# Output products of a strided plane made for two batches at once, with a new order of steps

## The chip, the core and the metric

The kernel runs on one NeuronCore of one Trainium2 chip. The metric is device time in microseconds of one execution. The engines are named as in the profile: PE (TensorE, matmuls; PEld are its weight loads), DVE (VectorE), ACT (ScalarE), POOL (GpSimd) and SP (SyncE, which only issues transfers here). Each engine works through its own list of instructions in order and waits on semaphores for the others.

## What is computed

Linear attention with a learned feature map, followed by a gated causal convolution unit. Cut to what matters:

```python
batch, n_heads, seq, head_dim, d_feat = 8, 8, 576, 64, 128

def phi(x):                                     # x: q or k
    proj = np.einsum('bhsd,df->bhsf', x, w_phi)
    proj = proj - np.max(np.abs(proj), axis=-1, keepdims=True)
    return np.concatenate([np.exp(proj), np.exp(-proj)], axis=-1)

q_p, k_p = phi(q), phi(k)
kv = np.einsum('bhsf,bhsd->bhfd', k_p, v)
z = np.sum(k_p, axis=2)
num = np.einsum('bhsf,bhfd->bhsd', q_p, kv)
den = np.einsum('bhsf,bhf->bhs', q_p, z)[..., None] + 1e-06
x = (num / den).transpose(0, 2, 1, 3).reshape(8, 576, 512)

gate_pre = sum(conv_w[t] * xp[:, t:t + 576] for t in range(5))   # causal, xp is x padded by 4
out = (1 / (1 + np.exp(-gate_pre)) * (x @ w_val)) @ w_out
```

## The kernel before

**Tiling.** Row s of a sequence is split as s = 9 r + j, with r from 0 to 63 and j from 0 to 8: nine "planes" j of 64 rows each. The work is cut into 32 units, four per batch, each a pair of heads on the 128 partitions. Planes 0 to 7 of a unit are handled together, two planes per product. Plane 8 of a batch is left over; it is done once per batch, for all eight heads, by the steps whose names begin with h.

**Steps of a unit.** T transposes k and q on PE into PSUM, Tc copies them to on-chip memory (Tk, Tq, Tkc and Tqc are the halves for unit 0). PK and PA project k and q with tokens on the partitions. mK and mQ take the maximum magnitude per row on DVE, NG negates it on POOL, and E takes its exponential on ACT. Kp and Km are the two exponentials of the keys on ACT; V scales v by E on POOL; KV is the product of keys and values on PE, and KM its copy. PQ projects q with features on the partitions, SH subtracts the maxima there by a product with a negative identity, Qp and Qm are the two exponentials. NUM is numerator and denominator, XN the division on DVE. XQ (PE transposes) with XC (a copy), or XP (a transposing transfer on SP's queue), turn the result to have channels on the partitions, in one of two XT buffers.

**Steps of a batch.** HL copies a one-row shifted edge inside XT on POOL. GA makes the convolution as products with diagonal matrices DIAG, built once by DG0 to DG3 from the taps (CW holds them); TH is the tanh of the gate, VAa and VAb are the value products, GV is the gated value on DVE, OUT the output products, four of 128x512 per group of 128 rows, OE the eviction with a factor of one half, ST the stores. For plane 8 the same is done by hGA, hVA, hTH, hGV, hOUT, hOE and hST. LX and LY make a permuted copy of the output weights, WX one of the value weights.

**Where plane 8's output products stand.** A batch has only 64 rows in plane 8. hOUT therefore makes 64 output partitions at a time: for each of four blocks of input channels two products, one for each half of the output columns, with the halves on partitions 0 to 63 and 64 to 127 of one bank:

```python
PS[x * 64:x * 64 + 64, bank[0], 0:256],
m.hGV[:, jt // 2, (jt % 2) * R:(jt % 2 + 1) * R], wout(jt, x * 256, x * 256 + 256),
```

**Order.** A string, ORDER, lists every step with its number, its PSUM banks after @ and, where there is a choice, its engine after a colon (P is POOL, D DVE, A ACT, S SP). The program issues the steps in that order, so it sets the order on every engine. `Lk`, `Lq` and `Lv` are loads of a batch: a single digit is the batch, 11 is plane group 1 of batch 0, 12 groups 2 and 3; LV and LO load the two weight matrices. POOL issues most of them, so they take places in POOL's list. Z1 is a filler: one product of zeros that keeps PE busy. Steps that read the same PSUM banks on two engines keep the order of the list.

## Time and profile before

| | us |
|---|---|
| runs shown | 228.06, 228.54, 232.13 |
| median of these | 228.54 |
| the profiled execution | 227.52 |
| span of its records | 225.7 |

The profile shows the profiled execution only, by the span's own clock from 0. A group's row gives its count, its busy time and the mean of one instruction in ns, then the idle time of the engine just before it and what ended that. "Busy" of PE includes the pipelined end of each matmul, so neighbouring groups overlap. The chain of waits is followed back from the last instruction; each piece in it has its start, its length, and its engine, tile and line.

### The profile page before, as it was taken

How to read it: one execution, taken by the hardware profiler on the slowest of the kernel's cores; microseconds unless marked ns; L12 is line 12 of the kernel's file. 1: busy time of each engine (PE TensorE's matmuls, PEld its weight loads, DVE VectorE, ACT ScalarE, POOL GpSimd, SP SyncE). 2: the span in 40 equal slices, each digit the busy share in tenths (PEclk: the TensorE clock that was granted, in tenths of full speed). 3: DMA queues.
4: the chain of work that ended last, by engine and by line, in shares of the span. 5: the costliest groups of instructions: out<-in, count | busy, mean ns of one | idle time of the engine just before them, and what ended most of it. 6: DMA issues, size and time to landing. Idle time of an engine off the chain costs nothing.

```text
span 225.7 us, 10552 instructions
## 1 busy us (share of the span) xinstructions
PE 208.0 (92%) x4667; PEld 137.0 (61%) x4667; DVE 182.9 (81%) x291; ACT 190.0 (84%) x290; POOL 120.1 (53%) x177
## 2 busy tenths in 40 slices
PE   7738898999999999998998999999999999999991
PEld 2325666666757556755756676766675677577550
DVE  1699989988997998969895999889976998683361
ACT  3488999999999898897996899899999989979241
POOL 7198986664876338726646427832672564640101
PEclk9967999999999999999999999999999999999999
DMA  6999998060994993519998994089427545600456
GB/s 178 262 209 207 207 208 143 6 105 8 161 156 99 174 165 78 126 24 162 186 132 225 140 126 124 9 157 180 72 36 126 121 89 126 156 13 3 112 125 184
DMA packets 30823, 28.90 MB, mean 128 GB/s; under 512 B 12245, under 2 KB 25941, under 8 KB 30778
## 3 DMA queue, kind: packets, MB, share of 16 engines
q0 software_dynamic: 13024, 14.45, 41.5%
q1 hardware_dynamic: 17290, 13.19, 26.9%
q8 instruction: 36, 0.59, 1.1%
q10 hardware_dynamic: 464, 0.59, 1.0%
q14 instruction: 9, 0.07, 0.1%
HBM read 30.48 MB, written 9.44 MB: 177 GB/s over the span
## 4 chain that ended last, share of the span: by engine, by line
PE 60%; DVE 9%; ACT 9%; DMA 9%; issue 8%; POOL 2%; POOLq 0%; SPq 0%; DVEq 0%; ACTq 0%
PE PS L854 10%; PE PS L890 8%; PE PS L380 7%; PE PS L514 6%; PE PS L608 5%; PE PS L537 5%; DMA XT<-XN 4%; PE PS L822 4%; DMA kN<-in_k_dram 3%; PE PS L328 3%; ACT QT L581 3%; PE PS L528 3%; ACT KT L465 3%; DMA out_dram<-hOS 2%; DVE MQ L395 2%
## 5 line engine op out<-in xcount | busy, mean ns | idle before, releaser
L487 POOL TENSOR_TENSOR VT<-vN,E 128x1024 bf16<-128x1024 bf16 x28 | 53.3, 1905 | 29.1 <-ACT E L442 28.8
L465 ACT ACTIVATE KT<-PS 128x1024 bf16<-128x1024 f32 x64 | 64.0, 1036 | 2.8 <-DVE MK L395 1.5
L581 ACT ACTIVATE QT<-PS 128x1024 bf16<-128x1024 f32 x64 | 62.3, 1032 | 4.6 <-PE PS L537 4.6
L395 DVE TENSOR_REDUCE MK<-PS 128x8 f32<-128x1024 f32 x32 | 39.0, 1220 | 8.9 <-PE PS L380 5.3
L395 DVE TENSOR_REDUCE MQ<-PS 128x8 bf16<-128x1024 f32 x32 | 38.9, 1217 | 0.8 <-PE PS L380 0.5
L890 PE MATMUL PS<-WOX,GV 128*128 128x512 bf16 x96 | 26.0, 379 | 0.0
L436 POOL TENSOR_SCALAR MK<-MK 128x8 f32<-128x8 f32 x32 | 7.5, 236 | 34.6 <-DVE MK L395 28.9
L380 PE MATMUL PS<-W,T 64*128 64x128 bf16 x512 | 24.4, 220 | 1.3 <-DVE T L207 0.7
L854 PE MATMUL PS<-XT,WVX 128*128 128x512 bf16 x96 | 24.7, 380 | 0.4 <-issue 0.2
L514 PE MATMUL PS<-VT,KT 64*128 64x65 bf16 x1024 | 22.5, 191 | 1.7 <-DVE XN L619 0.5
L880 DVE SCALAR_TENSOR_TENSOR GV<-GATE,PS 128x512 bf16<-128x512 bf16 x32 | 21.0, 681 | 2.9 <-PE PS L854 2.4
L619 DVE TENSOR_TENSOR XN<-PS,RCP 128x512 bf16<-128x512 f32 x32 | 22.1, 691 | 1.3 <-DVE RCP L618 0.2
L514 PEld LDWEIGHTS <-KT 64*128 64x128 bf16 x1024 | 19.0, 94 | 6.5 <-issue 1.4
L380 PEld LDWEIGHTS <-T 64*128 64x128 bf16 x512 | 16.1, 95 | 9.7 <-issue 5.2
L608 PE MATMUL PS<-KVS,QT 128*128 128x65 bf16 x512 | 21.5, 193 | 0.1
L608 PEld LDWEIGHTS <-QT 128*128 128x128 bf16 x512 | 19.3, 98 | 3.3 <-issue 1.5
L537 PE MATMUL PS<-nident,MQ 128*128 128x128 bf16 x256 | 19.8, 220 | 0.0
L832 ACT ACTIVATE GATE<-PS 128x1024 bf16<-128x1024 f32 x15 | 14.6, 1031 | 5.6 <-PE PS L822 5.6
L207 DVE COPY T<-PS 128x1024 bf16<-128x1024 bf16 (+1 forms) x25 | 16.8, 673 | 2.4 <-PE PS L328 2.3
L537 PEld LDWEIGHTS <-MQ 128*128 128x128 bf16 x256 | 14.4, 98 | 5.6 <-issue 4.4
L890 PEld LDWEIGHTS <-GV 128*128 128x128 bf16 x128 | 11.1, 97 | 10.8 <-DVE GV L880 0.4
L618 DVE RECIPROCAL RCP<-PS 128x8 f32<-128x8 f32 (+1 forms) x40 | 7.9, 198 | 10.1 <-PE PS L608 9.5
(100 smaller groups left out, 390.5 us busy)
## 6 DMA issues: line engine op xcount, KB each, us to landing
out_dram<-OS SPq DMA_DIRECT2D x28, 256.0 KB, 3.9
qN<-in_q_dram POOLq DMA_DIRECT2D x7, 576.0 KB, 9.2
kN<-in_k_dram POOLq DMA_DIRECT2D x7, 576.0 KB, 7.8
vN<-in_v_dram POOLq DMA_DIRECT2D x7, 576.0 KB, 7.8
vF<-in_v_dram SPq DMA_DIRECT2D x2, 576.0 KB, 8.5
out_dram<-hOS SPq DMA_DIRECT2D x14, 64.0 KB, 3.2
out_dram<-OS SPq DMA_DIRECT2D x6, 128.0 KB, 2.5
WVAL<-in_moe_w_val_dram POOLq DMA_DIRECT2D x1, 512.0 KB, 12.1
```

The lines of the kernel that those rows point to most:

```text
L380: nc.tensor.matmul(PS[:, bank[jj], x * P:(x + 1) * P], t(r, x), W2[r, :], start=True, stop=True,)
L395: nc.vector.tensor_reduce(dst, x, AX.X, ALU.max, apply_absolute_value=True)
L465: nc.scalar.activation(o, x, AF.Exp, scale=1.0 if ft == 0 else -1.0)
L487: e.tensor_tensor(dst[:, :, :, 0:D], x.unsqueeze(1).to_broadcast([P, 2, n, D]), E[:, :, :].unsqueeze(3).to_broadcast([P, 2, n, D]), ALU.mult,)
L514: nc.tensor.matmul(PS[:, bank[h], ft * E1:(ft + 1) * E1], w, x, start=(c == 0), stop=(c == 8),)
L537: nc.tensor.matmul(PS[:, u.PQ[jj], :].rearrange("p (h x r) -> p h x r", h=2, x=4)[:, :, x, :], u.MQ[:, jj, x:x + 1].to_broadcast([P, P]), ...
L581: nc.scalar.activation(o, x, AF.Exp, scale=1.0 if ft == 0 else -1.0)
L608: nc.tensor.matmul(PS[:, bank[x // 2], y * E1:(y + 1) * E1], u.QT[:, ft, h * 4 + x, :, :].rearrange("p j r -> p (j r)"), u.KVS[:, h, ft * ...
L619: nc.vector.tensor_tensor(dst, nv[:, :, :, 0:D], rv.unsqueeze(3).to_broadcast([P, n, 4, D]), ALU.mult,)
L854: nc.tensor.matmul(PS[:, m.val[jt], :], wval(dt, jt), XTs[m.b % 2][:, dt, 4 * R:12 * R], start=(dt == 0), stop=(dt == 3),)
L880: nc.vector.scalar_tensor_tensor(out=m.GV[:, jt, :], in0=m.GATE[:, jt, :], scalar=1.0, in1=PS[:, m.val[jt], :], op0=ALU.add, op1=ALU.mult,)
L890: nc.tensor.matmul(PS[:, m.out[x], :], m.GV[:, jt, x * P:(x + 1) * P], wout(jt), start=(jt == 0), stop=(jt == 3),)
```

## The change

Batches 0 to 5 are taken in pairs (PAIRED = 3 pairs). Both batches of a pair write their gated plane 8 into one tile, hGV, laid out so that for each block of 128 channels the 64 rows of the even batch and the 64 of the odd one are next to each other. The odd batch's step hOUTm then makes four products of 128x512 for both, hOEm evicts 128x512 in one step into a tile of its own pool, and hSTm stores it by two transfers of 64 rows with all 512 columns. hOUT, hOE and hST of batches 0 to 5 are gone; batches 6 and 7 keep theirs. `seen`, `behind`, `between` and the steps SHt and hSHt are added to the code, but no step of the list uses them.

```diff
@@ op_hGV
-        m.hGV = pools["hGV"].tile([P, 2, 2 * R], BF16, name="hGV")
+        if PAIRED and b % 2 and b < 2 * PAIRED:
+            m.hGV = batches[b - 1].hGV
+        else:
+            m.hGV = pools["hGV"].tile([P, 2, 2, 2, R], BF16, name="hGV")
+        o = m.hGV[:, :, :, b % 2, :]
+        g = m.hGATE[:, :, :].rearrange("p a (c r) -> p a c r", r=R)
+        v = banks(m.hG)[:, :, 2 * R:4 * R].rearrange("p a (c r) -> p a c r", r=R)
         nc.vector.scalar_tensor_tensor(
-            out=m.hGV[:, :, :], in0=m.hGATE[:, :, :], scalar=1.0, in1=banks(m.hG)[:, :, 2 * R:4 * R],
-            op0=ALU.add, op1=ALU.mult,
+            out=o, in0=g, scalar=1.0, in1=v, op0=ALU.add, op1=ALU.mult,
         )
@@ op_hOUT
-                    m.hGV[:, jt // 2, (jt % 2) * R:(jt % 2 + 1) * R], wout(jt, x * 256, x * 256 + 256),
+                    m.hGV[:, jt // 2, jt % 2, b % 2, :], wout(jt, x * 256, x * 256 + 256),
@@ new steps
+    def op_hOUTm(b, bank):
+        m = batches[b]
+        m.hout = bank[0]
+        for jt in range(4):
+            nc.tensor.matmul(
+                PS[:, bank[0], :], m.hGV[:, jt // 2, jt % 2, :, :].rearrange("p b r -> p (b r)"), wout(jt),
+                start=(jt == 0), stop=(jt == 3),
+            )
+
+    def op_hOEm(b, eng):
+        m = batches[b]
+        m.hOS = pools["hOSm"].tile([P, DM], FP32, name="hOSm")
+        half(eng, m.hOS[:, :], PS[:, m.hout, :])
+
+    def op_hSTm(b, eng):
+        for x in range(2):
+            engines[eng].dma_start(
+                out[b - 1 + x].rearrange("(r j) o -> r j o", j=J)[:, 8, :],
+                batches[b].hOS[x * 64:x * 64 + 64, :],
+            )
@@ ORDER, its first two lines
-XZ0:D Z1@0 Z1@0 Lq11:P Z1@0 Z1@0 Z1@0 Z1@0 Z1@0 Z1@0 Lk11:P Z1@0 CK0 Tk0@0,1 W0 Z1@2 Z1@2 CQ0 Z1@2
-Tq0@2,3 Lv13:S Tqc0:D Tkc0:A PA0@0,1 PK0@2,3 LC0 ND0:D Lk12:P Lv12:S T1@4,5 mQ0 mK0 Lq12:P PQ0@6,7
+Z1@0 Z1@0 XZ0:D Z1@0 Lk11:P CQ0 Z1@0 ND0:D Z1@0 Z1@0 Z1@0 XZ1:D Lq11:P Z1@0 Z1@0 CK0 Z1@0 Z1@0 W0 Z1@0
+Z1@0 Tk0@0,1 Lv13:S Tq0@2,3 Z1@4 LC0 Z1@4 Tkc0:D Tqc0:D Z1@7 PQ0@0,1 PA0@2,3 mQ0 PK0@6,7 Km0 Lk12:P
```

ORDER is a new list throughout: the steps keep their meaning, but their places, banks and, for 41 of them, their engines differ. Fillers number 28 in place of 27. Among the steps that change engine: Tkc0, Tc1, KM0, LY3, hTc1 and XC0 go from ACT to DVE, hTc0 and WX2 from DVE to ACT, DG1 and WX1 from DVE to POOL, WX3 from POOL to ACT. The rest are evictions and copies that change sides between ACT and DVE in both directions.

DVE's list at the start of the program, before. MQ and MK are the maxima, W the projection weights, T and hT the transposed inputs, DIAG the diagonal matrices, cwT the taps.

```order
L226 CAST kN<-kF 128x576
L232 CAST W_161<-wtmp 128x128
L207 COPY T<-PS 128x2x4x64
L220 TENSOR_SCALAR nident<-ident_bf 128x128
L395 TENSOR_REDUCE MQ<-PS 128x8
L395 TENSOR_REDUCE MK<-PS 128x8
L207 CAST ident_159<-ident_bf 5x5
L395 TENSOR_REDUCE MK<-PS 128x8
L395 TENSOR_REDUCE MQ<-PS 128x8
L245 TENSOR_SCALAR cwT<-PS 128x20
L260 TENSOR_TENSOR DIAG<-ident_bf,cwT 128x5x32 x4
L207 COPY hT<-PS 128x512
```

The same place now:

```order
L226 CAST kN<-kF 128x576
L232 CAST W_164<-wtmp 128x128
L207 COPY T<-PS 128x2x4x64 x2
L395 TENSOR_REDUCE MQ<-PS 128x8
L207 COPY T<-PS 128x2x8x64
L207 CAST ident_162<-ident_bf 5x5
L395 TENSOR_REDUCE MK<-PS 128x8 x2
L245 TENSOR_SCALAR cwT<-PS 128x20
L395 TENSOR_REDUCE MQ<-PS 128x8
L207 COPY T<-PS 128x2x8x64
L395 TENSOR_REDUCE hMQ<-PS 128x4
```

Both halves of unit 0's transposes and those of unit 1 are copied by DVE now, and the DIAG row and the copy of hT have left this place.

POOL's list for the first units, before. VT and hVT are the scaled values of V and hV, vF is batch 0's v, the 128x16 and 128x8 casts belong to V and hV.

```order
L487 TENSOR_TENSOR VT<-vF,E 128x16x64
L491 CAST VT<-E 128x16
L272 DMA qN<-in_q_dram 128x4x576
L272 DMA vN<-in_v_dram 128x4x576
L687 TENSOR_SCALAR hMK<-hMK 128x4
L272 DMA vN<-in_v_dram 128x4x576
L487 TENSOR_TENSOR hVT<-vF,hE 128x8x64
L491 CAST hVT<-hE 128x8
L487 TENSOR_TENSOR VT<-vF,E 128x16x64
L491 CAST VT<-E 128x16
L260 TENSOR_TENSOR DIAG<-ident_bf,cwT 128x5x32 x4
L260 TENSOR_TENSOR DIAG<-ident_bf,cwT 128x5x64 x2
```

The same place now:

```order
L487 TENSOR_TENSOR VT<-vF,E 128x16x64
L491 CAST VT<-E 128x16
L260 TENSOR_TENSOR DIAG<-ident_bf,cwT 128x640
L487 TENSOR_TENSOR VT<-vF,E 128x16x64
L491 CAST VT<-E 128x16
L260 TENSOR_TENSOR DIAG<-ident_bf,cwT 128x5x32 x4
L707 TENSOR_SCALAR hMK<-hMK 128x4
L260 TENSOR_TENSOR DIAG<-ident_bf,cwT 128x5x64 x2
L487 TENSOR_TENSOR hVT<-vF,hE 128x8x64
L491 CAST hVT<-hE 128x8
```

Three groups of DIAG (DG0, DG3, DG2) now stand ahead of hV0, which stood before them; the loads that stood here have moved ahead of the first V.

POOL's list around unit 13, before; numbers are those of the tiles. VT_2330, VT_2484 and VT_2615 are the values of units 12, 13 and 14, hVT_2421 those of plane 8 of batch 3; XT0_168 is the edge copy of batch 2.

```order
L487 TENSOR_TENSOR VT_2330<-vN_351,E_2274 128x16x64
L491 CAST VT_2330<-E_2274 128x16
L436 TENSOR_SCALAR MK_2291<-MK_2291 128x8
L487 TENSOR_TENSOR hVT_2421<-vN_351,hE_2319 128x8x64
L491 CAST hVT_2421<-hE_2319 128x8
L487 TENSOR_TENSOR VT_2484<-vN_351,E_2413 128x16x64
L491 CAST VT_2484<-E_2413 128x16
L436 TENSOR_SCALAR MK_2474<-MK_2474 128x8
L207 COPY XT0_168<-XT0_168 128x4x4x63
L487 TENSOR_TENSOR VT_2615<-vN_351,E_2521 128x16x64
```

The same place now; VT_2489 belongs to unit 13 and VT_2579 to unit 14:

```order
L487 TENSOR_TENSOR VT_2489<-vN_1432,E_2384 128x16x64
L491 CAST VT_2489<-E_2384 128x16
L272 DMA qN_2495<-in_q_dram 128x4x576
L436 TENSOR_SCALAR MK_2487<-MK_2487 128x8
L207 COPY XT0_173<-XT0_173 128x4x4x63
L487 TENSOR_TENSOR VT_2579<-vN_1432,E_2524 128x16x64
```

The load of batch 4's q, which had stood behind unit 10's values, now stands behind unit 13's.

## The prediction, made before the changed kernel ran

> **What bounds the kernel now.** I read the page's head first, then busy time by stage, then what the matmul engine waits for between the start and the last batch, then the chain of waits and the order of time in the first 30 us. The page:

> ```profile
> span 225.7 us, 10552 instructions
> PE 208.0 (92%) x4667; PEld 137.0 (61%) x4667; DVE 182.9 (81%) x291; ACT 190.0 (84%) x290; POOL 120.1 (53%) x177
> PE 60%; DVE 9%; ACT 9%; DMA 9%; issue 8%; POOL 2%; POOLq 0%; SPq 0%; DVEq 0%; ACTq 0%
> ```

> PE carries 60% of the chain that ends last. Three stretches by busy time (the columns are the stretch, PE, PEld, DVE, ACT, POOL, PE's clock), and the sum of the six batches between the first tap products of batch 0 and those of batch 6:

> ```profile
> 0.00:22.60 22.60, 15.30 (x221) 8.27 (x222) 15.24 (x25) 14.07 (x21) 15.20 (x27) 0.85 1.05 214
> 22.60:45.10 22.50, 20.00 (x497) 14.48 (x494) 21.58 (x38) 22.00 (x34) 17.31 (x28) 1.00 0.83 141
> 203.10:225.70 22.60, 17.79 (x254) 10.13 (x252) 8.72 (x18) 9.35 (x17) 2.04 (x5) 0.99 0.42 106
> sum 148.91, PE 145.91 PEld 97.56 DVE 131.24 ACT 137.34 POOL 79.77; mean PE 24.32 PEld 16.26 DVE 21.87 ACT 22.89 POOL 13.30
> ```

> So there are two limits. In the middle PE works 145.91 of 148.91 us: only PE work that is taken out, or a new PE wait, moves the end. In the start it is ACT and DVE: from 22.6 to 45.1 us ACT works 22.00 of 22.50, DVE 21.58, while PE has gaps. What the start gains is passed to the end, because PE runs without a hole from there. The longest wait of PE from 40 to 212 us:

> ```profile
> PE PS L822 <- issue: 0.6, 1, 0.6
> ```

> No PE wait there is longer than 0.6 us, so there is no stall in the middle for a new order to remove.

> **The change, part by part.** First the matmuls of plane 8. The chain of waits has hOUT (eight 64-column products), an ordinary OUT (four of 128x512, the shape that hOUTm has) and, from a closer window of the same chain, one filler product of zeros:

> ```profile
> 90.64 0.56 PE PS L977 x8
> 91.81 0.86 PE PS L890 x4
> 125.71 0.32 PE PS L213
> ```

> Six hOUT cost 6 x 0.56 = 3.36 us, three hOUTm 3 x 0.86 = 2.58: PE loses 0.78 us, all in the stretch where PE is the limit. Against it the new list has one filler more among the PE-bound batches (four in place of three after the first tap products): +0.32. Together -0.46.

> [...]

> The evictions:

> ```profile
> L903 ACT ACTIVATE OS<-PS 128x512 f32<-128x512 f32 x14 | 8.4, 624 | 2.8 <-PE PS L890 2.8
> L903 ACT ACTIVATE hOS<-PS 128x256 f32<-128x256 f32 x6 | 2.4, 401 | 0.7 <-PE PS L977 0.5
> L905 DVE TENSOR_SCALAR hOS<-PS 128x256 f32<-128x256 f32 x2 | 0.8, 413 | 0.0
> ```

> Six hOE were four on ACT and two on DVE (4 x 0.40 + 2 x 0.41); three hOEm on ACT are 3 x 0.62. ACT +0.27, DVE -0.83, neither on the path in the middle; if they were, -0.83 to +0.27 bounds it, and I take 0. The hGV write now goes in runs of 64 with a gap: no row shows such a write. Its price lies between 0 and, if gaps doubled it, 8 x 0.4 us on DVE; it resembles most the same shape without gaps, and I take 0, covered by the 17.7 us that DVE is idle in the 148.91. The stores are six fewer on SP's queue, with the same bytes; SP waits for data most of the time, so 0, between a fraction of a microsecond gained and lost at the end of the last store, which isn't one of them.

> Now the start. Its pieces in order of time (the chain first: DG1, and batch 0's tap products, which end the start; then single instructions, with the idle time before them and who ended it in square brackets):

> ```profile
> 13.39 2.74 DVE DIAG L260 x4
> 46.65 1.28 PE PS L822 x80
> ```
> ```profile
> 1.17 4.02 PE L213 MATMUL PS<-zt 128*128 128x512 bf16 x9 [1.17 <-DVE zt L173]
> 5.71 1.26 PE L213 MATMUL PS<-zt 128*128 128x512 bf16 x3
> 13.35 0.23 ACT L442 ACTIVATE E<-MK 128x16 f32<-128x16 f32 x1
> 16.52 0.39 PE L380 MATMUL PS<-W,hT 64*128 64x128 bf16 x4 [2.24 <-DVE hT L207]
> 17.68 1.08 ACT L700 ACTIVATE hKT<-PS 128x512 bf16<-128x512 f32 x2 [1.37 <-DVE hMK L395]
> 29.53 1.94 ACT L581 ACTIVATE QT<-PS 128x1024 bf16<-128x1024 f32 x2
> 90.73 0.26 POOL L491 CAST VT<-E 128x16 bf16<-128x16 f32 x1
> ```

> In the old order DG1 holds DVE for 2.74 us from 13.39, hTc0 stands behind it, PE then waits 2.24 us and ACT 1.37. The new order builds DG1 on POOL in unit 4 and copies hTc0 on ACT. The prices of the copies that change engines:

> ```profile
> L205 ACT ACTIVATE T<-PS 128x1024 bf16<-128x1024 bf16 x7 | 7.2, 1028 | 3.0 <-PE PS L328 3.0
> L205 ACT ACTIVATE KVS<-PS 128x260 bf16<-128x260 f32 x20 | 7.9, 397 | 3.2 <-PE PS L514 2.7
> L205 ACT ACTIVATE XT<-PS 128x512 bf16<-128x512 bf16 x6 | 3.7, 614 | 0.0
> L205 ACT ACTIVATE XT<-PS 128x256 bf16<-128x256 bf16 x5 | 1.9, 387 | 0.0
> L205 ACT ACTIVATE hT<-PS 128x512 bf16<-128x512 bf16 x3 | 1.8, 604 | 0.0
> L205 ACT ACTIVATE WOX<-PS 128x512 bf16<-128x512 f32 x1 | 0.7, 666 | 0.0
> L207 DVE COPY WVX<-WVAL 128x256 bf16<-128x256 bf16 x2 | 1.7, 883 | 0.0
> L207 DVE COPY WVX<-WVAL 128x128 bf16<-128x128 bf16 x4 | 0.8, 252 | 0.0
> L207 DVE COPY T<-PS 128x512 bf16<-128x512 bf16 x1 | 0.4, 424 | 1.4 <-PE PS L328 1.4
> L260 POOL TENSOR_TENSOR DIAG<-ident_bf,cwT 128x160 bf16<-128x160 bf16 x4 | 1.7, 447 | 0.0
> L260 POOL TENSOR_TENSOR DIAG<-ident_bf,cwT 128x320 bf16<-128x320 bf16 x2 | 1.4, 714 | 0.0
> L260 POOL TENSOR_TENSOR DIAG<-ident_bf,cwT 128x640 bf16<-128x640 bf16 x1 | 1.2, 1246 | 0.0
> L487 POOL TENSOR_TENSOR VT<-vF,E 128x1024 bf16<-128x1024 f32 x4 | 7.8, 1939 | 1.1 <-ACT E L442 1.1
> ```

> I follow ACT up to the end of unit 3's query exponentials (31.47 now), where ACT has no hole left. From its list go KM0 (0.40), LY3 (0.67), hTc1 (0.60) and XC0 (0.61), 2.28 us; hTc0 (0.60) and WX2 come. No row shows WX2 on ACT: two ACT copies of 256 columns are 0.77, two of DVE's are 1.77; it reads on-chip memory as the second does, but runs on the engine of the first, so I take 0.8. Net -0.9. The copies Tc1 (1.03) and Tkc0 (0.6) leave ACT too, but there ACT had nothing else ready: I cost that at 0. The 1.37 us wait goes. What is late instead: four more fillers of 0.43 each (1.26 / 3) stand ahead of the first transposes, but the three that stood between the two halves now stand behind both, so the second half comes as early as before; then both halves are copied on DVE one after the other (0.42 more) and the first maxima start about 0.5 later. And hE0 on ACT now waits for hNG0, which stands on POOL behind DG3: about 0.6. So -0.9 - 1.37 + 0.5 + 0.6 = -1.2. WX2's dearer price would leave -0.2, and a start without the two new delays would have -2.3; I take -0.9, a third of the way from -1.2 to the dear price. DVE's own list falls further up to there (DG1 2.74, WX2 1.77, against Tc1, Tkc0, KM0, hTc1 and XC0), so it does not decide, but for hmK0, which stands behind ACT's hKm0.

> The loads of batch 1 and WOR are now issued before unit 0's maxima. On POOL's queue they stand behind everything that the first units need, so I cost them at 0. In the last batch the order of the output products changes, but PE's list from batch 6's tap products to the last product is the same work, and the last eviction and store are the same: 0, within 0.7 (a pair of moved copies).

> **The sum.** -0.46 - 0.9 = -1.4 against the profiled execution, whose own time was 227.52 us around a span of 225.7: 226.1. The median of the runs shown is 228.54, 1.0 above it; on that scale I forecast 227.2.

> **Rivals.** (1) *The start loses: POOL becomes its limit.* In the new order POOL does V0, DG0, V1, DG3, hNG0, DG2 and hV0 before KV1 and KV0 can run, and PA3, PQ2 and SH2 stand behind these on PE. From E0 (13.35 + 0.5): two V with their columns 2 x (1.94 + 0.26), DG0 1.25, DG3 4 x 0.45, DG2 2 x 0.71, hV0 half of a V, 1.1, and the small NG: 24.0. KV1, KV0 and what follows to SH2 I estimate at 2.4, from the same groups in the old chain, so unit 2's exponentials can start at 26.4; ACT's own list gets there at about 27 by the working above. The room is some 0.6 us: with POOL 1.5 later the start's gain is gone (228.1), and each further microsecond is one lost. With POOL 3.5 later: 230.1. For it: these two times are nearly equal. Against it: POOL's rows are steady here.

> (2) *A late load stalls PE.* Batch 4's q is issued some 3 units later, right after V13. Now V13 ends at 90.99 (the POOL row above, 90.73 + 0.26) and hT4, the first reader, starts at 100.23 in the chain:

> ```profile
> 100.23 0.34 PE PS L655 x8
> ```
> ```profile
> qN<-in_q_dram POOLq DMA_DIRECT2D x7, 576.0 KB, 9.2
> kN<-in_k_dram POOLq DMA_DIRECT2D x1, 576.0 KB, 12.8
> ```

> The lead is 9.2 us, the median landing of a q load too; the slowest load took 12.8, among others. This decides once the landing passes 9.2: up to +3.6, 230.8. Against it: only one load is in flight there.

> (3) *DVE's relief reaches the end.* Over the run DVE loses about 4.2 us (DG1 2.74, hOE 0.83, WX1's four copies 0.8; the other copies that are exchanged cancel to some tenths). If DVE were the hidden limit, 228.54 - 4.2 - 0.46 = 223.9. Against it: ACT is busier everywhere.

> (4) *New waits in the middle.* The whole list is new. Now PE is idle 3.0 us of the 148.91; twice that gives 230.2, three times 233.2.

> **How the numbers follow.** My forecast has 0.50 (its own range 225.5 to 229.5), rival 1 0.20 (229 to 233.5), rival 2 0.10 (228 to 230.8), rival 3 0.12 (222.5 to 225), rival 4 0.08 (230 to 234). The range 223.5 to 231.5 leaves out half of rival 3 and a third of rivals 1 and 4, with the forecast's tails under 0.2. Two per cent, about what a measurement of this kernel tells from no change, lies at 223.97 and 233.11: faster 0.09 (most of rival 3), slower 0.09 (the ends of 1 and 4 and what I don't see), within 0.82.

> **What would show it.** hOUTm at 0.86 us in the chain; the end of unit 3's query exponentials near 30.6 in place of 31.47; the wait of PE for hT0 at 16.5 us moved to ACT's copy; the first tap products near 45.8; 25 us a batch after that; no PE wait above 1 us at hT4. The forecast is wrong if KV1 stands waiting for POOL past 24.5 us while ACT idles, or if PE's idle time between the first and the seventh tap products exceeds 4 us.

## The result and the profile after

The changed kernel takes 225.74 us (225.36 to 226.66), the kernel before 228.47 beside it: a ratio of 0.9892 [0.9851, 0.9933], so 2.5 us less (1.5 to 3.4). The forecast was 227.2, 1.4 us less. The change stays within two per cent, to which the forecast gave 0.82. The profiled execution took 225.96 us around a span of 224.1, so profile against profile the gain is 1.6 us. (42 steps change engine; the text ahead says 41.)

The page's head of the kernel after:

```profile
span 224.1 us, 10422 instructions
PE 204.9 (91%) x4593; PEld 137.1 (61%) x4632; DVE 179.8 (80%) x285; ACT 189.1 (84%) x289; POOL 121.3 (54%) x181
PE 66%; DVE 13%; ACT 7%; issue 4%; POOL 4%; DMA 4%; ACTq 1%; DVEq 0%; POOLq 0%
```

Its busy time between the first tap products of batch 0 and those of batch 6, by the same windows as before, and the line of PE's waits from 40 to 212 us that is largest in total (five of 0.16 us; no single wait in that stretch is longer than 0.3):

```profile
sum 146.98, PE 142.85 PEld 96.46 DVE 129.78 ACT 139.50 POOL 83.94; mean PE 23.81 PEld 16.08 DVE 21.63 ACT 23.25 POOL 13.99
```
```profile
PE PS L874 <- issue: 0.8, 5, 0.2
```

The six batches are 1.93 us shorter (148.91 before), where 0.46 was forecast. By its own words the forecast is wrong if PE is idle there for more than 4 us. The difference is 146.98 - 142.85 = 4.13, but 39 of the 4632 products have no record in this profile (4593 against 4632 weight loads), and the five waits of 0.16 us stand where the first product of a group has none; so PE's true idle time is less, and the sign does not decide. The start of the kernel after, from the chain of waits and the order of time on PE and ACT:

```profile
2.30 7.94 DMA qN<-in_q_dram
45.86 1.28 PE PS L842 x80
```
```profile
17.04 0.61 PE L380 MATMUL PS<-W,hT 64*128 64x128 bf16 x8 [0.38 <-ACT hT L205]
26.69 3.78 ACT L601 ACTIVATE QT<-PS 128x1024 bf16<-128x1024 f32 x4
```

PE's 2.24 us wait for hT0 is 0.38. The query exponentials of units 2 and 3 end at 30.47 (forecast 30.6, before 31.47), the tap products start at 45.86 (forecast 45.8, before 46.65). That agreement is luck: the first query load took 7.94 us here. The same rows of a second execution of the same kernel (n0_new_again), where it took 6.72:

```profile
2.31 6.72 DMA qN<-in_q_dram
44.51 1.28 PE PS L842 x80
```
```profile
25.29 3.79 ACT L601 ACTIVATE QT<-PS 128x1024 bf16<-128x1024 f32 x4
```

There the exponentials end at 29.08 and the tap products start at 44.51: the start gives 2.1 us, not 0.8. Of the seven profiles of the new list that are read below, four have their first tap products at 44.3 to 44.8 us, with the early loads in time. The other three (45.4 to 45.8) have one late load: the query load here, and in p4 and t1 the projection weights, which land at 7.4 us and not at 5.7 to 6.3. The seven profiles of the old list have 46.6 to 47.1. The pairs' products in the chain, their evictions and the write with gaps:

```profile
158.47 0.81 PE PS L1027 x3
```
```profile
L923 ACT ACTIVATE hOSm<-PS 128x512 f32<-128x512 f32 x3 | 1.9, 637 | 0.0
L993 DVE SCALAR_TENSOR_TENSOR hGV<-hGATE,PS 128x256 bf16<-128x256 bf16 x8 | 3.3, 416 | 0.3 <-ACT hGATE L981 0.2
```

The row has three of the group's four products; the first has no record here. Evictions and writes cost what the forecast said (637 ns against 624 an eviction, 416 a write as before's 417). The end of the run gives something back. The last output products and the last store that SP issues, before and after:

```profile
220.10 0.81 PE L890 MATMUL PS<-WOX,GV 128*128 128x512 bf16 x3
221.78 0.54 SPq L931 DMA_DIRECT2D out_dram<-OS  x1
```
```profile
217.25 0.81 PE L910 MATMUL PS<-WOX,GV 128*128 128x512 bf16 x3
220.84 0.55 SPq L951 DMA_DIRECT2D out_dram<-OS  x1
```

From the end of the last product to the end of the span it is 225.7 - 220.91 = 4.8 us before and 224.1 - 218.06 = 6.0 after. All profiles of the old list have 4.7 to 4.9 there and all of the new list 5.9 to 6.1.

### The profile page after: what moved, and what is told of

Same layout as the page of the kernel before. It is cut to its first block, busy times and chain, and to the rows that moved or that the text cites. A ratio compares the mean times of both kernels' runs of the same rounds, so it can differ in the third digit from the quotient of the medians.

```text
span 224.1 us, 10422 instructions
## 1 busy us (share of the span) xinstructions
PE 204.9 (91%) x4593; PEld 137.1 (61%) x4632; DVE 179.8 (80%) x285; ACT 189.1 (84%) x289; POOL 121.3 (54%) x181
## 4 chain that ended last, share of the span: by engine, by line
PE 66%; DVE 13%; ACT 7%; issue 4%; POOL 4%; DMA 4%; ACTq 1%; DVEq 0%; POOLq 0%
PE PS L910 12%; PE PS L874 9%; PE PS L514 7%; PE PS L628 6%; PE PS L380 6%; PE PS L537 5%; PE PS L842 5%; DVE MK L395 4%; DMA qN<-in_q_dram 4%; PE PS L528 3%; ACT KT L465 3%; DVE MQ L395 3%; PE PS L328 2%; PE PS L962 2%; POOL VT L487 2%
## 5 line engine op out<-in xcount | busy, mean ns | idle before, releaser
L487 POOL TENSOR_TENSOR VT<-vN,E 128x1024 bf16<-128x1024 bf16 x28 | 53.4, 1906 | 21.8 <-ACT E L442 21.6
L395 DVE TENSOR_REDUCE MK<-PS 128x8 f32<-128x1024 f32 x32 | 39.0, 1220 | 7.4 <-PE PS L380 6.3
L395 DVE TENSOR_REDUCE MQ<-PS 128x8 bf16<-128x1024 f32 x32 | 39.0, 1219 | 2.2 <-PE PS L380 1.8
L380 PE MATMUL PS<-W,T 64*128 64x128 bf16 x512 | 24.9, 223 | 0.9 <-DVE T L207 0.3
L910 PE MATMUL PS<-WOX,GV 128*128 128x512 bf16 x85 | 23.8, 379 | 0.8 <-issue 0.2
L874 PE MATMUL PS<-XT,WVX 128*128 128x512 bf16 x83 | 22.9, 380 | 1.1 <-issue 0.6
L380 PEld LDWEIGHTS <-T 64*128 64x128 bf16 x512 | 16.2, 97 | 11.9 <-issue 9.0
L514 PE MATMUL PS<-VT,KT 64*128 64x65 bf16 x1024 | 22.0, 191 | 0.4 <-DVE MK L395 0.3
L514 PEld LDWEIGHTS <-KT 64*128 64x128 bf16 x1024 | 18.8, 94 | 5.0 <-DVE MK L395 1.6
L207 DVE COPY T<-PS 128x1024 bf16<-128x1024 bf16 (+1 forms) x28 | 18.5, 666 | 3.4 <-PE PS L328 3.2
L537 PEld LDWEIGHTS <-MQ 128*128 128x128 bf16 x256 | 14.9, 99 | 5.4 <-issue 5.1
## 6 DMA issues: line engine op xcount, KB each, us to landing
kN<-in_k_dram POOLq DMA_DIRECT2D x7, 576.0 KB, 8.7
qN<-in_q_dram POOLq DMA_DIRECT2D x7, 576.0 KB, 8.1
vN<-in_v_dram POOLq DMA_DIRECT2D x7, 576.0 KB, 10.0
vF<-in_v_dram SPq DMA_DIRECT2D x2, 576.0 KB, 8.6
```

Source lines behind the costliest of these rows:

```text
L380: nc.tensor.matmul(PS[:, bank[jj], x * P:(x + 1) * P], t(r, x), W2[r, :], start=True, stop=True,)
L395: nc.vector.tensor_reduce(dst, x, AX.X, ALU.max, apply_absolute_value=True)
L487: e.tensor_tensor(dst[:, :, :, 0:D], x.unsqueeze(1).to_broadcast([P, 2, n, D]), E[:, :, :].unsqueeze(3).to_broadcast([P, 2, n, D]), ALU.mult,)
L514: nc.tensor.matmul(PS[:, bank[h], ft * E1:(ft + 1) * E1], w, x, start=(c == 0), stop=(c == 8),)
L537: nc.tensor.matmul(PS[:, u.PQ[jj], :].rearrange("p (h x r) -> p h x r", h=2, x=4)[:, :, x, :], u.MQ[:, jj, x:x + 1].to_broadcast([P, P]), ...
L874: nc.tensor.matmul(PS[:, m.val[jt], :], wval(dt, jt), XTs[m.b % 2][:, dt, 4 * R:12 * R], start=(dt == 0), stop=(dt == 3),)
```

## The experiments

This table holds for all of them. "Six batches" is the time from batch 0's tap products to batch 6's, read from PE's rows in order of time. A "hole" is a stretch of at least 0.25 us in which PE stands still and the profile shows nothing that it waits for (the row ends in "<-issue"), counted from 30 us on.

| kernel | median us | ratio to before | first tap products | six batches | holes |
|---|---|---|---|---|---|
| before | 228.47 | | 46.58 | 148.91 | 1, 0.58 us |
| after | 225.74 | 0.9892 [0.9851, 0.9933] | 45.79 | 146.98 | 0 |
| n0_new_again | 225.93 | 0.9914 [0.988, 0.9948] | 44.44 | 147.79 | 0 |
| e1_pairs_old_order | 229.73 | 1.0075 [1.0042, 1.0108] | 46.82 | 150.96 | 2, 2.52 |
| e2_half_products | 225.51 | 0.9894 [0.9857, 0.993] | | | |
| e5_pairs_twice | 227.65 | 0.9996 [0.9967, 1.0024] | 44.26 | 150.09 | 1, 0.42 |
| e3_v6_later | 228.29 | 1.0002 [0.9965, 1.0039] | 46.62 | 147.73 | 1, 0.43 |
| e4_dg1_pool | 227.56 | 0.9964 [0.9921, 1.0008] | 46.92 | 147.76 | 0 |
| e6_no_late_fillers | 225.30 | 0.9883 [0.9822, 0.9945] | 44.38 | 147.25 | 1, 0.25 |
| p1_pairs_old_half | 232.56 | 1.0187 [1.0124, 1.025] | 46.56 | 152.90 | 3, 3.35 |
| p2_pairs_old_full | 229.32 | 1.0036 [0.9993, 1.008] | 46.99 | 148.54 | 1, 0.43 |
| p3_before_half | 231.37 | 1.0151 [1.0094, 1.0208] | 47.08 | 151.95 | 4, 3.11 |
| p4_new_half | 231.28 | 1.0139 [1.009, 1.0187] | 45.79 | 152.66 | 7, 5.05 |
| t1_tail_stores | 224.85 | 0.9862 [0.9813, 0.9911] | 45.42 | 147.37 | 0 |

The profiled execution of e2 took 228.61 us, 3.1 above the median, so its stretches are left out; only its start is used above. It has four holes, of 0.77, 0.60, 0.55 and 0.34 us: the new list isn't free of them in every execution.

**n0_new_again**: the changed kernel as it is.

> The changed kernel itself, beside the other three of this call on one chip, as their base. Measured so far 225.74 against 228.47 of the kernel before, ratio 0.9892: 2.73 us less. All theories expect the same again, 0.986 to 0.993.

225.93 us. It sets the scale for what follows, and its profile shows the start without the late load.

**e1_pairs_old_order**: the new steps in the old list.

```diff
-... Qm13 mK14 hOUT0@0 V13:P ... NG14:P hOE0:D KM12:A ... XN13 hST0:S V14:P ...
+... Qm13 mK14 V13:P ... NG14:P KM12:A ... XN13 V14:P ...
-... OE9:D hOUT1@7 ST4:S ... E18 hOE1:A T19@5,6 ... NG19:P hST1:S GV13 ...
+... OE9:D hOUTm1@7 ST4:S ... E18 hOEm1:A T19@5,6 ... NG19:P hSTm1:S GV13 ...
```
(and so for batches 2 to 5)

> The old order with plane 8's products in pairs (the three pair steps at the odd batch's places). Theory A (PE's work is the limit of the middle): three products of 0.86 us in place of six of 0.56, 0.78 us less, 227.7 on the scale of 228.47, ratio 0.9966. Theory B (the gain of the middle comes with the pairs in some other way, by fewer evictions and stores): most of the 2.7 us, about 226.2, ratio 0.990. Theory C (products of plane 8 stand in holes of PE): 0.

229.73 us, 1.7 slower than before: pairing alone, in the old list, doesn't save 0.78 but loses. Its profile has two holes, the largest so far. PE's rows around them:

```profile
117.91 0.41 PE L513 MATMUL PS<-VT,KT 64*128 64x65 bf16 x16
119.84 0.20 PE L513 MATMUL PS<-hVT,hKT 64*128 64x65 bf16 x2 [1.52 <-issue]
124.94 0.40 PE L379 MATMUL PS<-W,T 64*128 64x128 bf16 x8 [1.00 <-issue]
```

They stand in the middle of a group of 36 products, and right behind the tap products: no step begins in the first place. The six batches are 2.05 us longer than before's, and the two holes are 1.94 longer than before's one (2.52 - 0.58). So the profile finds the loss in the holes, and not at the pairs' places in the list.

**e2_half_products**: the new list, each pair as sixteen 64x256 products.

```diff
-        for jt in range(4):
-            nc.tensor.matmul(PS[:, bank[0], :], m.hGV[:, jt // 2, jt % 2, :, :]..., wout(jt), ...)
+        for y in range(2):
+            for jt in range(4):
+                for x in range(2):
+                    nc.tensor.matmul(
+                        PS[x * 64:x * 64 + 64, bank[0], y * 256:y * 256 + 256],
+                        m.hGV[:, jt // 2, jt % 2, y, :], wout(jt, x * 256, x * 256 + 256), ...)
```

> The new order with each pair's four products of 128x512 made as sixteen of 64x256 into the same bank; eviction and stores move the same bytes. Theory A: 3 x (2 x 0.56 - 0.86) = 0.78 us more than the changed kernel. [...]

225.51 us, against 225.93 for the four wide products. The 0.78 us can't be seen in the time; the two intervals are each 1.6 us wide, so a fraction of it could be there.

**e5_pairs_twice**: the new list, each pair's products made twice (the second round has the same sums).

```diff
-        for jt in range(4):
+        for jt in (0, 1, 2, 3) * 2:
```

> The new order with each pair's four products made twice over: 3 x 0.86 = 2.58 us more work of PE, nothing else. Theory A: the changed kernel's time plus 2.2 to 2.6 us. If the middle were limited by latencies of DVE, ACT or transfers, with PE waiting in small holes, less than 1.3 us more.

227.65 us, 1.7 to 1.9 above n0 (by the medians and by the ratios), between the two expectations (2.2 to 2.6, and less than 1.3). In the profile the three stretches with a pair grow by 0.75, 0.87 and 0.80 us (from one batch's tap products to the next's: 24.93, 23.96 and 27.28 against n0's 24.18, 23.09 and 26.48), each near the 0.86 of one round. So in the profile PE's work counts almost one for one in the middle, and in the time about 0.7 for one. What hid the 0.78 us in e1 was larger than it; in e2 the 0.78 us can lie within the intervals.

**e3_v6_later** and **e4_dg1_pool**: two edits of the old list, the load of batch 6's v, and DG1 and hTc0 as the new list has them.

```diff
-... hKm4 hNG4:P Lv6:P PA16@2,3 ... NUM17@0,1 V18:P GA3@4,5,6,7 ...
+... hKm4 hNG4:P PA16@2,3 ... NUM17@0,1 V18:P Lv6:P GA3@4,5,6,7 ...
```
```diff
-... V0:P Lq2:P DG1:D hT0@2 hTc0:D hPK0@2,3 ... hPK1@2,3 NG4:P hKm1 ...
+... V0:P Lq2:P hT0@2 hTc0:A hPK0@2,3 ... hPK1@2,3 NG4:P DG1:P hKm1 ...
```

> The old kernel with one token moved: the load of batch 6's v, issued at 105.7 us just before batch 5's k and 4.5 us before the last transposing transfer of batch 3, is issued two units later. Theory D (in the old kernel the tap products of batch 3 start late because that transfer, 9.4 us long, lands late behind two loads): the transfer takes 5 to 7 us, the edge copy that waits for it comes 1 us or more earlier, the interval from batch 2's to batch 3's tap products falls from 25.1 to about 24, and the total by 0.8 to 1.3 us. Theory A alone (PE's work): no change, within 0.3 us.

> The old kernel with two steps changed in the start: DG1 goes from DVE to POOL, behind unit 4's sign change, and the copy hTc0 from DVE to ACT. My forecast's mechanism: DVE is free at 13.4 us, PE's wait of 2.24 us for hT falls under 1, unit 3's query exponentials end 0.5 to 1.2 us before 31.47, and the total falls as much. Rival (ACT's list is what limits the start, and gets 0.6 us more work): the wait goes but the exponentials end within 0.3 us of 31.47, total the same.

228.29 and 227.56 us: neither is a difference that the intervals show. Theory D isn't borne out: in e3 the interval from batch 2's to batch 3's tap products falls only from 25.06 to 24.72. In e4 PE's wait for hT0 falls to 0.69 and ACT ends unit 3's query exponentials earlier, and it is of no use:

```profile
29.11 1.97 ACT L578 ACTIVATE QT<-PS 128x1024 bf16<-128x1024 f32 x2
```
```profile
46.92 0.43 PE L819 MATMUL PS<-XT,DIAG 32*32 32x512 bf16 x16
```

They end at 31.08 against 31.47, and the tap products start at 46.92, no sooner than before's 46.58. So these two moves alone don't make the new start. But the two profiles serve for something else. They are executions of the old list with no hole (e4) and one of 0.43 (e3), both faster than their kernels' medians (226.66 and 226.32 us), and their six batches take 147.76 and 147.73 us. Those of the new list without a hole take 146.98, 147.79 and 147.37, 147.38 on the mean. The difference of 0.4 us agrees with the forecast's 0.46, but the three spread over 0.8 us, so it isn't shown by them.

**e6_no_late_fillers**: the new list without its four fillers behind the first tap products.

```diff
-... Lk4:P Z1@7 T13@4,5 ... VAb11 Z1@5 Km16 ... T21@4,5 Z1@0 hPA5@0,1 ... OE12:D Z1@0 hE5 ...
+... Lk4:P T13@4,5 ... VAb11 Km16 ... T21@4,5 hPA5@0,1 ... OE12:D hE5 ...
```

> The new kernel without the four filler products that stand behind batch 0's tap products. Theory A (PE is the limit there): 4 x 0.21 to 0.32 less, 0.9 to 1.3 us under the changed kernel. If they stand in holes in which PE waits anyway: the same.

225.30 us, 0.6 below n0, with intervals that overlap; four fillers of 0.32 would be 1.28. In the middle PE has several new waits of 0.4 to 0.7 us for DVE and ACT, so part of the fillers stood where PE would have waited.

**The pieces of PE's program.** Where do the holes stand? Number PE's weight loads and products in the order of the built program, from 0. Then before's hole lies ahead of number 5050, and e1's two ahead of 4794 and 5050:

```
before 5050 L822 LDWEIGHTS DIAG_167
e1     4794 L513 LDWEIGHTS hKT_2922
e1     5050 L379 LDWEIGHTS T_3318
```

5050 - 4794 = 256, and both are 186 more than a multiple of 256. (The expectations below count two less: 4792, 5048, and 184 and 56 for 186 and 58.) The page of the profile has a DMA queue that the kernel doesn't use by itself; before's row, and that of p3_before_half, whose list is longer:

```profile
q8 instruction: 36, 0.59, 1.1%
```
```profile
q8 instruction: 37, 0.61, 1.1%
```

36 packets of 0.59 MB are 16 KB each. Before's list of PE has 9330 entries, so 36 of its numbers are of the form 186 + 256 k; p3's has 9458, and there are 37. The four kernels of this group bear the count out (9386 and 9388 entries have 36 packets, 9458 and 9514 have 37): in these profiles PE's instructions came in pieces of 256, by transfers of 16 KB. The DMA queues of e1 in two windows, 110 to 117.3 us and 117.3 to 118.7 (packets, MB, busy share):

```profile
q0 software_dynamic: 828, 0.93, 99.3%
q1 hardware_dynamic: 609, 0.15, 34.3%
```
```profile
q1 hardware_dynamic: 264, 0.07, 124.4%
q0 software_dynamic: 75, 0.08, 68.1%
q8 instruction: 1, 0.02, 5.5%
```

PE passes number 4538, the boundary ahead, at 112.0 us. For five microseconds no piece comes while loads fill the queues. Then one does, from 117.38 to 118.61, and PE, which reached 4794 at 118.3, goes on at 119.84.

The transfers of all 14 profiles, taken in order with the boundaries, tell when a piece was late. The transfer of a piece begins 1.1 us (median; at most 5.4) after PE has passed the boundary ahead and takes 1.0 us (median). At none of the 492 boundaries that can be paired so does PE go on sooner than 1.2 us after its end. At the 21 holes of the table it goes on 1.2 to 1.6 us after. So there was a hole where PE came through 256 instructions sooner than that. This happened in two ways. Ahead of nine holes PE took only 2.8 to 3.8 us for them (5.7 is the median), and loads were under a sixth of the DMA engines' time in the microsecond after PE had passed the boundary. Ahead of the other twelve loads took over half of it. Over all boundaries the transfer begins 0.8 us after PE's passing where loads take under 5% (299 of them) and 2.7 us after it where they take over 75% (150 of them), by the medians.

So a test: put every instruction of PE half a piece (128 places) or a whole piece (256) further back, with products at the start whose results nobody reads. The edit below is that of p1_pairs_old_half (on e1) and p3_before_half (on before): Y68 stands for four of the fillers. p4_new_half does the same on after, and p2_pairs_old_full (on e1) replaces eight fillers by Y136:

```diff
+    def op_Y(n, bank):
+
+        for _ in range(n):
+            nc.tensor.matmul(PS[0:32, bank[0], 0:32], zt[:, 0:32], zt[:, 0:32], start=True, stop=True)
...
-XZ0:D Z1@0 Z1@0 Lq11:P Z1@0 Z1@0 ...
+XZ0:D Y68@0 Lq11:P ...
```

> The kernel with the pairs in the old order (229.73 us, with two holes of 1.5 and 1.0 us in TensorE's row that nothing in the profile explains, both where 184 instructions more than a multiple of 256 lie behind TensorE), and 64 products more at its start: four of the fillers that keep TensorE busy while it waits for the first loads are replaced by 68 products of 32 columns, whose results nobody reads. So every later instruction of TensorE stands 128 places further back, half of a piece of 256. Theory I (TensorE's instructions come in pieces of 256 over a DMA queue of their own, 36 transfers of 16 KB in the profile, and the holes are pieces that come late): unexplained holes over 0.25 us lie only where the old numbering has 56 more than a multiple of 256, none at 4792 or 5048 of the old numbering, and the time moves from 229.7 by 0.7 us or more, down to 227.5 to 229.0 if the transfers come through between the loads there, up if not. Rival P (the places of the pairs in the old order make it slow): 229.7 within 0.5, with the losses at the same instructions. Pads: first tap products at 46.8 within 0.4.

> The same with 128 products more at the start (eight fillers replaced by 136 products of 32 columns): every later instruction of TensorE stands 256 places back, a whole piece, so the pieces begin at the same instructions of the program as without. Theory I: the time is again that of the pairs in the old order, 229.7 within 0.5, and unexplained holes lie at old numbers 184 more than a multiple of 256. Should the small products themselves cost or gain, this run shows it: then it differs from 229.7 as the run with half a piece does. Rival P: 229.7 within 0.5 too.

> The kernel before with 64 products more at its start in place of four fillers, so that its pieces of 256 instructions begin half a piece elsewhere. Theory I: holes move to old numbers 56 more than a multiple of 256, none at 5048 where the kernel before shows 0.58 us; the time moves by 0.5 us or more from 228.0, in the same direction as for the pairs in the old order with half a piece. Rival (the 0.58 us hole is chance and the order alone makes the difference): 228.0 within 0.4.

> The changed kernel with 64 products more at its start: four of its first fillers are replaced by 68 products of 32 columns, so that TensorE's pieces of 256 instructions begin 128 places elsewhere in the program, as was done with the kernel before (228.35 to 231.37 us) and with the pairs in the old order (229.7 to 232.6). The question is whether the changed kernel's freedom from late pieces comes from its order or from where its pieces happen to begin. Theory B (where the pieces begin): the time rises by 1 to 3 us, to 227 to 229, and unexplained holes of 0.5 us and more stand in TensorE's row at old numbers 56 more than a multiple of 256, most likely in the batches between 70 and 76 us and between 107 and 142 us. Rival O (the new order asks for its pieces when the transfers are less busy): 225.9 within 0.7, no hole over 0.4 us. First tap products at 44.5 within 0.4 (45.8 if the first query load is late again).

Half a piece makes e1 2.8 us slower (232.56), before 3.0 slower (231.37) and the changed kernel 5.4 slower (231.28); by the ratios it is 2.6, 3.4 and 5.1. A whole piece, with twice the small products, leaves e1 where it was (229.32, within the intervals); this was tried on e1 alone. The holes move too. PE's rows in p1, p3 and p4, the largest of each:

```profile
74.66 0.29 PE L518 MATMUL PS<-VT,KT 64*128 64x65 bf16 x7 [1.17 <-issue]
140.65 0.28 PE L384 MATMUL PS<-W,T 64*128 64x128 bf16 x3 [1.16 <-issue]
162.34 0.26 PE L632 MATMUL PS<-KVS,QT 128*128 128x65 bf16 x3 [1.02 <-issue]
```
```profile
75.43 0.29 PE L516 MATMUL PS<-VT,KT 64*128 64x65 bf16 x7 [1.10 <-issue]
128.54 0.21 PE L516 MATMUL PS<-VT,KT 64*128 64x65 bf16 x2 [1.00 <-issue]
```
```profile
52.54 0.29 PE L332 MATMUL PS<-ident_bf,kN 64*128 64x64 bf16 x7 [1.02 <-issue]
76.38 0.29 PE L518 MATMUL PS<-VT,KT 64*128 64x65 bf16 x7 [1.21 <-issue]
141.00 0.34 PE L384 MATMUL PS<-W,T 64*128 64x128 bf16 x6 [1.17 <-issue]
```

In the kernels' own lists these eight lie ahead of 3002, 5818, 6842; 3002, 5306; 1978, 3002 and 5818, and each is 186 more than a multiple of 256. So are all 21 holes in the table and the four of e2. Two more stops at such numbers, 0.97 us in p1 and 0.67 in p3, are put down to another engine by the profile. Theory I and theory B hold, with the sign left open for p1 and p3 and the size of p4 too small (1 to 3 us expected). Between the profiled executions of p4 and n0 (231.6 and 225.35 us) 1.35 us lie in the start (first tap products 45.79 against 44.44, with one late load and a hole of 0.47 at 36 us) and 4.9 in the six batches.

At half a piece the old list takes 231.37 us and the new one 231.28. There the change shows no gain; the two intervals leave room for some 1.7 us either way.

**t1_tail_stores**: two of the last stores of the new list on POOL's queue.

```diff
-... hOE7:A hST7:A OE28:A SO28:SS OUb29 ...
+... hOE7:A hST7:P OE28:A SO28:SP OUb29 ...
```

> The changed kernel, with two of its last stores moved: the two 64 KB stores of batch 7's plane 8 (hST7) go from ACT's queue to POOL's, and the second store of OE28's planes from SP's queue to POOL's. In the changed kernel's profile the last product ends at 218.06, but 6.04 us pass until the end of the span (4.79 before), ACT issues hST7 for 1.17 us ahead of its last two evictions, and SP's last store is issued at 220.84, 2 us behind the last eviction. Theory T (the queues that issue the last stores took back what the rest gained): the stretch from the last product to the end goes from 6.0 to 4.6 to 5.0 us and the time falls by 0.9 to 1.5 us, to about 224.7 us. Rival (the end is set by how long stores take to land): the stretch stays within 0.3 us of 6.0, and the time at 225.9.

224.85 us, the fastest kernel here, with an interval that overlaps n0's. The last issues on each queue:

```profile
215.54 3.88 SPq L951 DMA_DIRECT2D out_dram<-OS  x5
```
```profile
217.93 1.05 POOL L951 DMA_DIRECT2D out_dram<-OS  x2
218.75 0.53 ACTq L951 DMA_DIRECT2D out_dram<-OS  x1
```

The last store is issued by 219.42 and not 221.39, yet the span still ends 5.9 us behind the last product: by the profile the rival is right, by the median theory T. In the trace SP's last wait for its stores ends at 222.90 and not at 223.22, but POOL's closing wait, now behind three stores more, ends at 223.19 and not at 221.93: the profile shows the end passed on from SP to POOL. Why the median fell all the same stays open.

## Why the prediction came out as it did

The direction was right, the size was half of what came. The start was the right place; that the middle has no stall to lose was wrong.

- *PE products, -0.78, and a filler, +0.32.* The recorded products take what was said, and e5 shows that PE's time counts. Profiles with one small hole or none differ by 0.4 us in the middle, less than they spread. The term agrees with the runs, but no run shows it alone: neither the pairs in the old list nor the halves in the new one moved the time by it.
- *The start, -0.9.* Mis-sized: 2.1 where the first query load isn't late, 0.8 in the profiled run where it is 1.2 us late. In n0 ACT ends unit 3's query exponentials 2.4 us sooner, which is the sum without the delays that the forecast added (-2.3). The 0.5 for later maxima didn't come: E0 starts at 12.24, and started at 13.35 before. The 0.6 for hE0 was 0.1: ACT is done at 19.74, and hE0 starts at 19.83. The third of the way to WX2's dear price was not needed either: WX2 on ACT cost 0.75 for both copies, near the 0.8 of its cheap end. The rows of n0:

```profile
12.24 0.21 ACT L442 ACTIVATE E<-MK 128x16 f32<-128x16 f32 x1
18.71 1.03 ACT L465 ACTIVATE KT<-PS 128x1024 bf16<-128x1024 f32 x1
19.83 0.21 ACT L712 ACTIVATE hE<-hMK 128x8 f32<-128x8 f32 x1
24.68 0.75 ACT L205 ACTIVATE WVX<-WVAL 128x256 bf16<-128x256 bf16 x2
```

- *"There is no stall in the middle for a new order to remove."* This step failed. Before's row with 0.6 us of "issue" was quoted and passed over as too small. It was a piece of PE's program that came late: its transfer ended at 121.30 us, and PE went on at 122.76. Six batches of 148.91 against 147.76 in e4, which has no hole, put the loss at 1.15 us in the profiled execution; the hole of 0.58 and two shorter stops at boundaries (0.24 and 0.18) are 1.00 of that. The loss changes from execution to execution: the profiles of e1 and p2, whose pieces begin at the same instructions, have 2.52 and 0.43 us of holes. That this makes most of the spread of the kernel before (226.4 to 230.3 us in 75 of its 80 runs) is likely, but not shown, since few of the runs have a profile.
- *The last batch, 0 within 0.7.* Wrong: 1.25 us more from the last product to the end, less 0.13 gained between batch 6's tap products and the last product. "The last eviction and store are the same" failed: SP's last store is issued 2 us behind the last eviction there, and 0.2 before.
- Rival 1 was half right: the chain of the new start runs over POOL's V and DIAG, but KV1 starts at 23.47, ahead of the 24.0 worked out. Rival 2 didn't come: no wait of PE at hT4. Rival 3 didn't either, and rival 4, new waits in the middle, came with p4 and not with the change as it is.

The two profiles add up without a rest: -0.8 for the start, -1.9 for the six batches, -0.1 up to the last product, +1.25 for the end, -1.6 in all. For the medians the parts can only be put together from several executions: -2.1 for the start, -0.4 for the middle's work, -1.15 for late pieces and what they delay, +1.1 for the end: -2.55, against 2.5 (1.5 to 3.4) measured. The term -1.15 comes from single executions and -0.4 from a spread twice as wide, so that close agreement is partly luck.

What stays open: how much of the 2.5 us is late pieces in a usual execution. That loads hold a piece up is read from the traces alone; no run took the loads away at a boundary. A kernel that places its boundaries on purpose wasn't tried, nor were other shifts than half a piece and a whole one.

## What to carry to other kernels

On a kernel that PE bounds, a row that ends in "<-issue" in the middle of a group of products is worth a look: count PE's instructions up to it, and see whether the number is the same modulo 256. Such stops came where PE ran through a piece in 2.8 to 3.8 us (nine of the 21), or where loads took over half of the DMA engines' time when it entered one (twelve). Before crediting a new order with a gain, or blaming it, run old and new with the boundaries shifted by half a piece; here that moved the time by 2.8 to 5.4 us, more than the change. And a term of the start should be read from more than one execution, since one late load can hide it: here, with a query load of 7.94 us in place of 6.72, the start's gain read 0.8 us in place of 2.1.
